# Loading q, k and v sixteen subtiles at a time instead of eight in an attention and gated feed-forward kernel

## The chip, the cores and the metric

The kernel runs on one core of a Trainium2 chip. The metric is the device time of one execution in microseconds (us), as a median over several runs, and less is better. TensorE is called PE, VectorE is DVE and ScalarE is ACT; POOL is GpSimd, which issues the loads, and SP issues the stores.

## The reference

The inputs are float32: q, k and v of 4 batches x 6336 rows x 256 channels, two 256 x 256 weights and a bias.

```
qn = q / (norm of q over the 6336 rows);  kn = k / (norm of k likewise)
a  = softmax(kn.T @ qn / tau)            # 256 x 256 for each batch
x  = v @ a
H  = relu(x @ w_h);  T = sigmoid(x @ w_t + b_t)
out = T * H + (1 - T) * x                # float32
```

All of q and k of a batch must be read before its 256 x 256 matrix is known; only then can the first row of that batch's output be made.

## The kernel before

A batch is cut into subtiles of 128 rows, 48 of them and a short tail of two. Each load is a cast from float32 in HBM to float16 in SBUF, of CH = 8 subtiles: 128 partitions x 8 x 256 x 4 bytes, 1.049 MB read, 8 KB in a row per partition. *Stage one* takes the subtiles of q and k of one batch and sums the products k.q, k.k and q.q in PSUM (for 40 subtiles of batches 1 to 3 the squares of q go to ACT and POOL instead). After the last of them a short chain makes the softmax and folds the weights into it. *Stage two* takes v of that batch in pairs of subtiles: transposes, then three groups of four matmuls (h, t and d), relu and gate on ACT, product and result on DVE, and a store for every eight subtiles. From then on PE mixes stage two of one batch with stage one of the next.

What runs when is decided while the kernel is built. A list scheduler in the kernel, called the planner below, plays the whole program through with a fixed duration for each instruction and two DMA queues, and issues instructions in the order that this gives. Its constants (priorities, when a load is due) were found by search.

```python
CH = 8
QK_BUFS = 5
V_BUFS = 5
UNTIL = 73      # stores are held back until this pair of stage two
AHEAD = 16      # transposing DMAs of the last batch, pairs ahead
V_AHEAD = 2
PRIO = {"tr": (24.974, 16.445, 34.195, 63.304), ...}   # 12 rows, cut
...
class Plan:
    RATE = 424e3
    ...
            act = [qq for qq in queues.values() if qq and qq[0][2] <= t + eps]
            share = self.RATE / max(1, len(act))     # an even share for each queue
...
    def load(nm, b, j, s, n):
        ...                                          # the tail, cut
        if s == 0:
            tiles[(nm, b, j)] = new(nm, [P, CH, C], f16, f"{nm}{b}_{j}")
        t = tiles[(nm, b, j)]
        nc.gpsimd.dma_start(
            out=t[:, s : s + n, :], in_=main_rows(src)[:, j * CH + s : j * CH + s + n, :]
        )
...
    seq = []                                         # the order of the loads
    for b in range(B):
        for j in range(NJ + 1):
            if (b, j) != (0, 0):
                seq.append((NP * b + CH // 2 * j - V_AHEAD, 1, "v", b, j))
            if b >= 1 and (b, j) != (1, 0):
                at = slot_of((b - 1) * NS + CH * j)
                seq.append((at, 0, "q", b, j))
                seq.append((at, 0, "k", b, j))
    seq.sort(key=lambda x: (x[0], x[1]))
    for _, _, nm, b, j in seq:
        plan_load(nm, b, j)
```

The loads go out in the order of `seq`. An instruction on a subtile waits for the load that brings it, and a buffer is free when its last subtile has been used.

## Time and profile before

| kernel before | |
|---|---|
| time, median of three runs | 270.38 us (270.2 to 270.92) |
| span of the profiled run | 268.3 us |
| PE busy | 246.4 us, 92% |
| ACT, DVE, POOL busy | 73%, 68%, 49% |
| main loads of q, k and v, in pieces | 80 |

The prediction shows the slices, the waits and PE's order. Two further views matter for it. The first line below is the first part of the page (busy us, share of the span, number of instructions); then comes the loads' queue from the third part (packets, MB, share of the 16 engines' span), and last two groups of DMA issues (count, KB each in SBUF or HBM, median us from issue to landing).

```profile
PE 246.4 (92%) x2430; PEld 216.6 (81%) x2430; DVE 181.6 (68%) x377; ACT 195.1 (73%) x365; POOL 131.7 (49%) x167
...
q0 software_dynamic: 13472, 39.20, 75.0%
...
out_dram<-o SPq DMA_DIRECT2D x23, 1024.0 KB, 9.6
v<-in_v_dram POOLq DMA_DIRECT2D x24, 512.0 KB, 16.6
```

PE has the smallest reserve. A load takes far longer to land (16.6 us) than it takes the queue to carry it (2.465 us, worked out in the prediction), because several stand in line.

### The profile page before, as it was taken

How to read it: one execution, taken by the hardware profiler on the slowest of the kernel's cores; microseconds unless marked ns; L12 is line 12 of the kernel's file. 1: busy time of each engine (PE TensorE's matmuls, PEld its weight loads, DVE VectorE, ACT ScalarE, POOL GpSimd, SP SyncE). 2: the span in 40 equal slices, each digit the busy share in tenths (PEclk: the TensorE clock that was granted, in tenths of full speed). 3: DMA queues.
4: the chain of work that ended last, by engine and by line, in shares of the span. 5: the costliest groups of instructions: out<-in, count | busy, mean ns of one | idle time of the engine just before them, and what ended most of it. 6: DMA issues, size and time to landing. Idle time of an engine off the chain costs nothing.

```text
span 268.3 us, 6249 instructions
## 1 busy us (share of the span) xinstructions
PE 246.4 (92%) x2430; PEld 216.6 (81%) x2430; DVE 181.6 (68%) x377; ACT 195.1 (73%) x365; POOL 131.7 (49%) x167
## 2 busy tenths in 40 slices
PE   0697977999999999999999999999999999999991
PEld 0596864889989978999999878999998778888880
DVE  1000035777766789557878797586878998998994
ACT  1001016978888789999898887787798999998980
POOL 7233468688778064695689138567655110000000
PEclk9999999999999999999999999999999999999998
DMA  6999999999999999999999999999999999999995
GB/s 107 215 211 208 206 206 202 212 213 214 214 213 212 213 214 255 247 263 269 275 286 258 267 267 254 249 236 281 287 280 239 284 214 304 379 399 165 351 423 232
DMA packets 24622, 67.24 MB, mean 251 GB/s; under 512 B 9104, under 2 KB 11280, under 8 KB 21648
## 3 DMA queue, kind: packets, MB, share of 16 engines
q0 software_dynamic: 13472, 39.20, 75.0%
q1 hardware_dynamic: 11120, 27.64, 29.0%
q8 instruction: 19, 0.31, 0.4%
q14 instruction: 11, 0.09, 0.1%
HBM read 78.38 MB, written 25.95 MB: 389 GB/s over the span
## 4 chain that ended last, share of the span: by engine, by line
PE 76%; DMA 12%; ACT 5%; POOL 2%; issue 2%; DVE 2%; ACTq 0%; DVEq 0%; POOLq 0%
PE h L800 16%; PE t L800 16%; PE d L800 15%; PE sg L452 12%; DMA k<-in_k_dram 10%; PE sg L453 6%; PE vtps L760 5%; DMA v<-in_v_dram 2%; ACT uu L854 2%; PE sg L455 2%; PE t L831 1%; PE vtps L754 1%; PE ah L689 1%; POOL q L327 1%; ACT d L840 1%
## 5 line engine op out<-in xcount | busy, mean ns | idle before, releaser
L800 PEld LDWEIGHTS <-vtsb 128*128 128x128 f16 (+1 forms) x1044 | 98.8, 99 | 17.3 <-issue 3.2
L452 PE MATMUL sg<-q,k 128*128 128x256 f16 x384 | 83.8, 277 | 12.7 <-DMA k<-in_k_dram 12.6
L861 DVE SCALAR_TENSOR_TENSOR pp<-uu,d 128x512 f32<-128x512 f32 (+1 forms) x100 | 68.0, 684 | 28.4 <-PE d L800 16.1
L453 PE MATMUL sg<-k 128*128 128x128 f16 x384 | 76.8, 223 | 0.0
L854 ACT ACTIVATE uu<-t 128x512 f32<-128x512 f32 (+1 forms) x100 | 59.7, 597 | 19.1 <-PE t L800 18.5
L880 DVE SCALAR_TENSOR_TENSOR o<-h,pp 128x512 f32<-128x512 f32 x96 | 65.5, 686 | 1.7
L840 ACT ACTIVATE d<-h 128x512 f32<-128x512 f32 (+1 forms) x100 | 57.9, 584 | 5.7 <-PE h L800 4.9
L800 PE MATMUL t<-mr,vtsb 128*128 128x256 f16 (+1 forms) x348 | 52.2, 272 | 1.5 <-ACT t L533 1.2
L800 PE MATMUL h<-mr,vtsb 128*128 128x256 f16 (+1 forms) x348 | 51.2, 272 | 0.5 <-ACT vtsb L533 0.5
L800 PE MATMUL d<-mr,vtsb 128*128 128x256 f16 (+1 forms) x348 | 51.5, 272 | 0.1
L452 PEld LDWEIGHTS <-k 128*128 128x128 f16 x384 | 38.0, 99 | 16.7 <-DMA k<-in_k_dram 13.9
L476 POOL TENSOR_TENSOR sq<-sq,sq 128x1024 f32<-128x1024 f32 x15 | 35.4, 2361 | 16.7 <-ACT sq L470 16.6
L453 PEld LDWEIGHTS <-k 128*128 128x128 f16 x384 | 38.0, 99 | 1.5
L533 ACT COPY t<-bias_all 128x512 f32<-128x512 f32 (+1 forms) x60 | 35.4, 591 | 1.4
L455 PE MATMUL sg<-q 128*128 128x128 f16 x144 | 32.5, 226 | 0.0
L470 ACT ACTIVATE sq<-q 128x1024 f32<-128x1024 f16 x30 | 31.3, 1053 | 0.0
L760 PE MATMUL vtps<-ident,v 128*128 128x128 f32 x144 | 27.8, 275 | 0.9 <-DMA v<-in_v_dram 0.6
L569 DVE SCALAR_TENSOR_TENSOR junk<-sg,ident 128x128 f32<-128x128 f32 x16 | 4.6, 288 | 33.2 <-PE sg L455 32.7
L535 DVE COPY vtsb<-vtps 128x256 f32<-128x256 f32 (+2 forms) x47 | 19.6, 418 | 7.0 <-PE vtps L760 6.7
L327 POOL DMA_DIRECT2D v<-in_v_dram x24 | 13.7, 571 | 18.9 <-PE vtps L760 11.7
L327 POOL DMA_DIRECT2D q<-in_q_dram x28 | 15.4, 552 | 15.1 <-DMA q<-in_q_dram 7.1
L327 POOL DMA_DIRECT2D k<-in_k_dram x28 | 15.3, 548 | 13.1 <-DMA k<-in_k_dram 9.2
(78 smaller groups left out, 249.5 us busy)
## 6 DMA issues: line engine op xcount, KB each, us to landing
out_dram<-o SPq DMA_DIRECT2D x23, 1024.0 KB, 9.6
v<-in_v_dram POOLq DMA_DIRECT2D x24, 512.0 KB, 16.6
q<-in_q_dram POOLq DMA_DIRECT2D x21, 512.0 KB, 16.2
k<-in_k_dram POOLq DMA_DIRECT2D x21, 512.0 KB, 18.0
q<-in_q_dram POOLq DMA_DIRECT2D x5, 256.0 KB, 9.6
k<-in_k_dram POOLq DMA_DIRECT2D x5, 256.0 KB, 8.9
out_dram<-o SPq DMA_DIRECT2D x2, 512.0 KB, 4.2
out_dram<-ot SPq DMA_DIRECT2D x4, 192.0 KB, 5.1
```

The costliest lines, as they stand in the source:

```text
L327: nc.gpsimd.dma_start(out=t[:, s : s + n, :], in_=main_rows(src)[:, j * CH + s : j * CH + s + n, :])
L452: nc.tensor.matmul(sg[c][:, 0:C], kc, qa, start=first, stop=False)
L453: nc.tensor.matmul(sg[c][:, C : C + P], kc, kc, start=False, stop=False)
L455: nc.tensor.matmul(sg[c][:, C + P : C + 2 * P], qa[:, cs], qa[:, cs], start=False, stop=last)
L476: add(out=sq, in0=sq, in1=other)
L533: nc.scalar.copy(out=out, in_=in_)
L760: nc.tensor.transpose(ps[:, u, 0:nr], v.bitcast(f32), ident0[0:nr, 0:nr])
L800: nc.tensor.matmul(out[0:nr, u, :], vt[u][kt][:, 0:nr], mr[kt][:, col * C : (col + 1) * C], **flags(u, kt))
L840: nc.scalar.activation(out=d[0:nr, :, :], in_=ps_t["h", b, i][0:nr, :, :], func=Act.Relu, scale=0.5)
L854: nc.scalar.activation(out=uu[0:nr, :, :], in_=ps_t.pop(("t", b, i))[0:nr, :, :], func=Act.Tanh, scale=-0.5)
L861: nc.vector.scalar_tensor_tensor(out=pp[0:nr, :, :], in0=el.pop(("uu", b, i))[0:nr, :, :], scalar=1.0, in1=ps_t.pop(("d", b, i))[0:nr, :, ...
L880: nc.vector.scalar_tensor_tensor(out=ot, in0=ps_t.pop(("h", b, i))[0:nr, :, :], scalar=0.0, in1=el.pop(("pp", b, i))[0:nr, :, :], op0=AluO ...
```

## The change

The intent: fewer, larger loads with longer rows. Each main load now brings LC = 16 subtiles, reads 2.097 MB and has 16 KB in a row per partition. Three buffers of 16 take the place of five of 8. The head (all of q and k of batch 0, the first eight subtiles of q and k of batch 1, the first eight of v) still comes in pieces of at most 8. All constants of the planner were searched anew.

```diff
+LC = 16
-QK_BUFS = 5
-V_BUFS = 5
+QK_BUFS = 3
+V_BUFS = 3
-UNTIL = 73
-AHEAD = 16
+UNTIL = 63
+AHEAD = 11
-V_AHEAD = 2
+V_AHEAD = 2.5
 PRIO = {
-    "tr": (24.974, 16.445, 34.195, 63.304),
+    "tr": (-3.282, -3.586, -4.565, -0.124),
...                                    (eleven more rows, all new; HEAD, TAIL and ENDS too)
-            tiles[(nm, b, j)] = new(nm, [P, CH, C], f16, f"{nm}{b}_{j}")
+            tiles[(nm, b, j)] = new(nm, [P, LC, C], f16, f"{nm}{b}_{j}")
...
-        for j in range(NJ + 1):
-            if (b, j) != (0, 0):
-                seq.append((NP * b + CH // 2 * j - V_AHEAD, 1, "v", b, j))
-            if b >= 1 and (b, j) != (1, 0):
-                at = slot_of((b - 1) * NS + CH * j)
-                seq.append((at, 0, "q", b, j))
-                seq.append((at, 0, "k", b, j))
+        for j in range(NL + 1):
+            s = CH if (b, j) == (0, 0) else 0
+            seq.append((NP * b + (LC * j + s) // 2 - V_AHEAD, 1, "v", b, j, s))
+            if b >= 1:
+                s = CH if (b, j) == (1, 0) else 0
+                at = slot_of((b - 1) * NS + LC * j + s)
+                seq.append((at, 0, "q", b, j, s))
+                seq.append((at, 0, "k", b, j, s))
...
-    for _, _, nm, b, j in seq:
-        plan_load(nm, b, j)
+    for _, _, nm, b, j, s in seq:
+        plan_load(nm, b, j, s, LC - s)
```

More of the change, by code (lines that the diff above doesn't have):

```diff
@@ L27 @@
 APART = 5
-V_AHEAD = 2
+V_AHEAD = 2.5
 PRIO = {
-    "tr": (24.974, 16.445, 34.195, 63.304),
-    "ev": (74.59, 73.008, 67.512, 50.704),
-    "h": (-53.39, -86.015, -64.208, -14.641),
-    "bias": (-28.394, 23.065, -1.772, 4.453),
-    "t": (4.111, -1.918, 67.766, 74.312),
-    "relu": (46.555, -20.175, -1.498, 14.915),
-    "x": (0.958, -19.433, 43.343, -6.4),
-    "gate": (-54.132, 37.28, -94.231, -112.222),
-    "prod": (-40.861, -10.819, -26.763, -55.482),
-    "res": (53.604, 18.42, 116.457, -9.113),
-    "s1": (117.419, 42.459, 84.45),
-    "sq": (-15.195, 72.384, 19.395),
+    "tr": (-3.282, -3.586, -4.565, -0.124),
+    "ev": (-5.167, 18.053, 2.859, 3.861),
+    "h": (-1.452, 1.255, 0.62, 0.556),
+    "bias": (0.123, 3.568, 2.664, -1.224),
+    "t": (0.41, -6.752, -6.651, 4.505),
+    "relu": (-0.38, -0.537, 0.533, 9.281),
+    "x": (-2.607, 1.406, -4.336, 2.432),
+    "gate": (4.912, 4.7, 2.362, -12.905),
+    "prod": (-10.208, -4.864, -4.947, -16.086),
+    "res": (-15.539, 3.312, -8.353, 6.716),
+    "s1": (2.894, 15.325, 6.393),
+    "sq": (-0.758, 4.066, 5.437),
 }
 POW = 0.75
-HEAD = 5.5
-TAIL = 66
+HEAD = 4
+TAIL = 63
 EV = BIAS = ("ACT", "DVE")
-ENDS = [18, 48.5, 62.25]
+ENDS = [15.75, 46.75, 59.75]
 class Ring:
@@ L249 @@
     NJ = S // CH
+    NL = S // LC
     TR = (N - P * S) // 2
@@ L318, in load @@
         src = src_of[nm][b]
-        if j == NJ:
+        if j == NL:
             t = new(f"tail_{nm}", [P, 2, C], f16, f"{nm}{b}_t")
@@ L324, in load @@
         if s == 0:
-            tiles[(nm, b, j)] = new(nm, [P, CH, C], f16, f"{nm}{b}_{j}")
+            tiles[(nm, b, j)] = new(nm, [P, LC, C], f16, f"{nm}{b}_{j}")
         t = tiles[(nm, b, j)]
         nc.gpsimd.dma_start(
-            out=t[:, s : s + n, :], in_=main_rows(src)[:, j * CH + s : j * CH + s + n, :]
+            out=t[:, s : s + n, :], in_=main_rows(src)[:, j * LC + s : j * LC + s + n, :]
         )
@@ L333, in sub @@
         if s < S:
-            return tiles[(nm, b, s // CH)][:, s % CH, :]
-        return tiles[(nm, b, NJ)][0:TR, s - S, :]
+            return tiles[(nm, b, s // LC)][:, s % LC, :]
+        return tiles[(nm, b, NL)][0:TR, s - S, :]
     def rows(s):
@@ L340, with plan_load @@
     ld = {}
-    def plan_load(nm, b, j, s=0, n=CH):
-        size = P * n * C * 4 if j < NJ else TR * 2 * C * 4
-        tag = nm if j < NJ else f"tail_{nm}"
+    def plan_load(nm, b, j, s=0, n=LC):
+        size = P * n * C * 4 if j < NL else TR * 2 * C * 4
+        tag = nm if j < NL else f"tail_{nm}"
         x = plan.add(
             "POOL", len(plan.tasks), 0.54, 0, [], lambda: load(nm, b, j, s, n),
-            take=[tag] if s == 0 else [], size=size * (1 if j < NJ and n > 2 else SHORT),
+            take=[tag] if s == 0 else [], size=size * (1 if j < NL and n > 2 else SHORT),
         )
@@ L355, in loaded @@
         if s >= S:
-            return [ld[(nm, b, NJ)][0]]
-        return [[x for x in ld[(nm, b, s // CH)] if x.first <= s % CH][-1]]
+            return [ld[(nm, b, NL)][0]]
+        return [[x for x in ld[(nm, b, s // LC)] if x.first <= s % LC][-1]]
     def drops(nm, b, s):
-        if s < S and s % CH == CH - 1:
-            return [(ld[(nm, b, s // CH)][0], nm)]
+        if s < S and s % LC == LC - 1:
+            return [(ld[(nm, b, s // LC)][0], nm)]
         if s == NS - 1:
-            return [(ld[(nm, b, NJ)][0], f"tail_{nm}")]
+            return [(ld[(nm, b, NL)][0], f"tail_{nm}")]
         return []
-    plan_load("q", 0, 0)
-    plan_load("k", 0, 0)
-    consts = plan.add("POOL", len(plan.tasks), 0.6, 1.5, [], constants)
-    consts.serial = True
-    for j in range(1, NJ - 2):
-        plan_load("q", 0, j)
-        plan_load("k", 0, j)
-        if j == 2:
-            for nm in "qk":
-                plan_load(nm, 0, NJ)
-            b_ld = [
-                plan.add("POOL", len(plan.tasks), 0.54, 0, [], lambda u=u: load_b(u), size=4000)
-                for u in range(2)
-            ]
-    for j, s, n in ((NJ - 2, 0, 4), (NJ - 2, 4, 4), (NJ - 1, 0, 4), (NJ - 1, 4, 2), (NJ - 1, 6, 2)):
-        plan_load("q", 0, j, s, n)
-        plan_load("k", 0, j, s, n)
+    for s in range(0, LC, CH):
+        plan_load("q", 0, 0, s, CH)
+        plan_load("k", 0, 0, s, CH)
+        if s == 0:
+            consts = plan.add("POOL", len(plan.tasks), 0.6, 1.5, [], constants)
+            consts.serial = True
+    for s in range(LC, S - LC, CH):
+        plan_load("q", 0, s // LC, s % LC, CH)
+        plan_load("k", 0, s // LC, s % LC, CH)
+    for nm in "qk":
+        plan_load(nm, 0, NL)
+    b_ld = [
+        plan.add("POOL", len(plan.tasks), 0.54, 0, [], lambda u=u: load_b(u), size=4000)
+        for u in range(2)
+    ]
+    for s, n in ((0, 8), (8, 4), (12, 2), (14, 2)):
+        plan_load("q", 0, NL - 1, s, n)
+        plan_load("k", 0, NL - 1, s, n)
     for s in range(0, CH, CH // 2):
@@ L394 @@
         x.late = 0.5
-    plan_load("v", 0, 0)
+    plan_load("v", 0, 0, 0, CH)
     ends = [(-1, HEAD)] + [(e, (n + 1) * NS) for n, e in enumerate(ENDS)]
@@ L433, in order_of @@
             return list(range(NS))
-        return [*range(3 * CH), *range(S, NS), *range(3 * CH, S)]
+        return [*range(S - LC), *range(S, NS), *range(S - LC, S)]
     def sg_tag(b, c):
@@ L468, in squares @@
         sq_t[b, j, half] = sq = new("sq", [P, CH // 2, C], f32, f"sq{b}_{j}_{half}")
-        qa = tiles[("q", b, j)][:, half * CH // 2 : (half + 1) * CH // 2, :]
+        s = CH * j + half * CH // 2
+        qa = tiles[("q", b, s // LC)][:, s % LC : s % LC + CH // 2, :]
         nc.scalar.activation(out=sq, in_=qa, func=Act.Square)
@@ L766, in transpose_chunk @@
         vt = new(tag, [P, n, 2, nr], f16, f"{tag}{b}_{j}")
-        src = tiles[("v", b, j)][0:nr, :, :].rearrange("p s c -> p (s c)")
+        s = j * CH % LC
+        src = tiles[("v", b, j * CH // LC)][0:nr, s : s + n, :].rearrange("p s c -> p (s c)")
         nc.sync.dma_start(out=vt.rearrange("c s kt n -> c (s kt) n"), in_=src, transpose=True)
@@ L944, in plan_stage1 @@
                 take=[sg_tag(b, n)] if n < 2 else [],
-                drop=([] if apart(b, s // CH) else drops("q", b, s)) + drops("k", b, s),
+                drop=([] if apart(b, s // LC * LC // CH) and s < S else drops("q", b, s)) + drops("k", b, s),
             )
             x.lat = x.pitch if n < NS - 1 else 0.66
-            if apart(b, s // CH) and s % CH == CH - 1:
-                plan.add("NONE", 0, 0, 0, [x] + part_ends[s // CH], None, drop=drops("q", b, s))
+            if s % LC == LC - 1 and apart(b, s // LC * LC // CH):
+                ends = [y for j in range(s // LC * LC // CH, s // CH + 1) for y in part_ends.get(j, [])]
+                plan.add("NONE", 0, 0, 0, [x] + ends, None, drop=drops("q", b, s))
             if n < 2:
```

## The prediction

> **What bounds the kernel now.** I read the page's slices first, then the waits, then TensorE (PE) in order of time around the first h product, then the DMA queue in short windows. Slices of the page:
>
> ```profile
> PE   0697977999999999999999999999999999999991
> DMA  6999999999999999999999999999999999999995
> GB/s 107 215 211 208 206 206 202 212 213 214 214 213 212 213 214 255 247 263 269 275 286 258 267 267 254 249 236 281 287 280 239 284 214 304 379 399 165 351 423 232
> ```
>
> Each digit is a fortieth of 268.3 us. PE is full from the seventh slice on; the DMA engines are full almost from start to end. GB/s counts what lands, and a load reads float32 and lands float16, so 213 landed is 426 read. Two resources are thus nearly used up at once, and what matters is whether PE ever lacks its data. Longest waits:
>
> ```profile
> PE sg L452 <- DMA k<-in_k_dram: 12.6, 5, 9.0
> ...
> PE vtps L760 <- DMA v<-in_v_dram: 0.6, 1, 0.6
> ```
>
> PE waits for q and k only at the head, while batch 0 streams in (9.0 us for the first pair of loads, 3.6 in the other four waits), and for v once. PE around the first product of the second stage:
>
> ```profile
> 44.77 0.41 PE L760 MATMUL vtps<-ident,v 128*128 128x128 f32 x2 [0.63 <-DMA v<-in_v_dram]
> 45.65 0.61 PE L800 MATMUL h<-mr,vtsb 128*128 128x256 f16 x4 [0.46 <-ACT vtsb L533]
> 46.10 0.60 PE L800 MATMUL t<-mr,vtsb 128*128 128x256 f16 x4
> ...
> 61.55 0.38 PE L760 MATMUL vtps<-ident,v 128*128 128x128 f32 x2
> 61.76 0.27 PE L452 MATMUL sg<-q,k 128*128 128x256 f16 x1
> ```
>
> The head ends at 45.65 us, when the first v has landed. From there PE works without a marked wait on a load until its last product at about 262.5. The later visible idle, from windows of 20 us, is 2.0 us in all (0.1 to 60, 0.2 to 80, 0.4 to 100, 0.9 between 140 and 160, 0.4 between 200 and 220). So any PE delay caused after 45.65 goes into the end, unless other gaps are given up for it.
>
> How the queue shares loads and stores, in windows of 1 us:
>
> ```profile
> 104.00:105.00 1.00, 1.00 (x12) 0.84 (x11) 1.00 (x3) 0.97 (x3) 0.58 (x1) 1.00 1.08 222
> ...
> 106.00:107.00 1.00, 1.00 (x11) 0.84 (x10) 1.00 (x3) 0.96 (x2) 1.00 (x1) 1.00 1.07 328
> ```
>
> The last number is GB/s. Loads alone land some 213. With a store under way the sum is 328: if the store takes s of 426, s + (426 - s)/2 = 328 gives s = 230, about half each. The store in question was issued at 101.04 and begins to show only after 105.
>
> **What the Trainium skill says.** "DMA: Bandwidth & Descriptors", section "Measured", gives 341 GB/s for a transfer of 1 MB and 425 for 16 MB. This trace disagrees for queued transfers: in the head, GpSimd's next issues, each held by an earlier load's landing, follow at 9.18, 11.70, 14.16, 16.59 and 19.04 us, so 9.86 / 4 = 2.465 us for a load that reads 1.049 MB, 425 GB/s. Loads of 1 MB that stand in line already run at the rate the page gives for 16 MB; rows of 16 KB instead of 8 KB have no rate left to win. Same page, "Queues, rings and completion order": an engine goes round-robin between queues "at packet granularity". The half each above, with 8 KB read per row in both queues, agrees. Same page, "Anatomy of one DMA": about 2.0 us fixed per transfer; here it is covered by the queue (the median v lands 16.6 us after issue), so fewer transfers save no such time.
>
> **The change, part by part.** The instruction orders of both kernels can be compared without running them.
> 1. *Issues.* Main loads fall from 28 + 28 + 24 = 80 to 19 + 19 + 13 = 51. At about 0.55 us each GpSimd saves 29 x 0.55 = 16 us of its 131.7. GpSimd is 49% busy and never the bound: 0 on the path.
> 2. *Work of PE.* Same matmuls, but 18 instead of 17 bias matmuls into t (TAIL 63 for 66). Counting an elementwise group of four products as 0.436 us and a bias matmul as about 0.2: +0.2 us. The vector and scalar work is the same within a few copies.
> 3. *Head.* Batch 0 is still loaded in pieces of 8, 4 and 2 subtiles, and the same bytes stand ahead of the first v: all q and k of batch 0, eight subtiles of q and k of batch 1, the weights. That v is now issued before the norm on GpSimd instead of after it (38.88), but it was the queue and not the issue that held it, so it lands at 44.6 again and the first h starts at 45.65 again: 0.
> 4. *After the head, the part that I think decides.* Order of loads before: v, q, k, v, q, k ... of 8 subtiles, 2.465 us each. Now, after v: 8 more of q and k (47.1, 49.6), 8 of v (52.0), then 16 each of q (57.0), k (61.9), v (66.8), q (71.8), k (76.7), v (81.6). PE in its new order, from 45.65: two and a half pairs (6 groups x 0.436 + 2 transposes x 0.215 = 3.0) bring it to 48.7, where it needs the k of 49.6: wait 0.9. Up to the first matmul on q and k subtile 16 it has 19 groups (8.28), 8 subtiles of stage one at 0.334 (2.67; four matmuls, from the trace) and 6 transposes (1.29): 12.2. So it is there at 45.65 + 0.9 + 12.2 = 58.8 and waits for k until 61.9. Before, PE at 61.9 had done 21 groups, 12 subtiles and 9 transposes; now 19, 8 and 6. Deficit: 2 x 0.436 + 4 x 0.334 + 3 x 0.215 = 2.9 us. Smaller loads gave PE both inputs alternately; the larger ones make it wait for a whole 16 of q and a whole 16 of k when it has v for the pairs only up to pair 7.
> 5. *Next loads.* After 61.9 some 5.2 us of work reach the need for v at 67.1 (lands 66.8); a further 9.6 reach k at 76.7 (lands 76.7); a further 5.6 reach v at 82.3 (81.6). No further wait, but no slack.
> 6. *Buffers.* Three of 16 hold 48 subtiles, five of 8 held 40: no less ahead on average. The hold on stores ends at pair 63 instead of 73, the transposing DMAs go out 11 pairs ahead instead of 16: with 1.4 us per pair near the end and a median landing of 6.1 us, 15 us is still enough.
>
> Sum: +2.9 + 0.2 = +3.1 us. Against it stand the gaps that PE has anyway: the same count of groups, subtiles and transposes from 45.65 to the end comes to about 210 us, while the trace takes 216.8; some 7 us are lost in small gaps while PE waits for ScalarE or VectorE. While PE starves, those two catch up, and the new order may have fewer such gaps. I credit 1 us (a choice, not a measurement): 270.4 + 3.1 - 1.0 = 272.5.
>
> **Rivals.**
> *The gaps decide.* The reordered priorities could win back two or three of the 7 us of small gaps and the 2.0 of visible idle; then starvation is covered: 268 to 270. For it: ScalarE and VectorE are at 73% and 68% over the span, with peaks near 90%, and order does matter. Against: the old order was tuned as well.
> *Loads push stores aside.* If engines alternate row by row, a load row of 16 KB against a store row of 8 KB leaves a store a third: a store of 1 MB takes 7.4 us instead of 5, after a longer wait for its turn. Stores landed in 9.5 us in the median and 18.0 at most; seven output buffers with five held leave about two chunks, some 17 us, for one to land. VectorE never waited for a store before; it might now: 274 to 277. Against: the load queue then runs dry sooner and gives the time back.
> *Nothing moves.* If the DMA total is the true bound (104.3 MB at 425 GB/s is 245 us, plus the transposing DMAs and the short pieces), a PE delay at 60 us is hidden behind stores at the end: 270. Against: stores catch up by 264 us, when PE is already done.
>
> **Range and chances.** The floor is head plus present work: 3 us better needs nearly half of the small gaps, so 2% faster (below 265.0) is hardly reachable: 4%. Slower by 2% (above 275.8) needs the starvation and a stall of stores together: 14%. The range runs from all starvation won back plus 2 us (268.5) to starvation plus some 3 us of stalls (276.0).
>
> **What would show it.** Step 4: a PE wait on the DMA of k near 59 to 62 us, of 2 to 3 us, and another below 1 us near 49. Step 3: first h at 45.6, within 0.5. Head and queue rate: still 213 GB/s landed between 46 and 95 us. Second rival: about 284 instead of 320 GB/s in windows where both queues run, stores landing later, VectorE's o waiting on the DMA of the output. If PE has no wait on loads after 50 us, or if the first h comes over 1 us earlier, my working is wrong.

## The result, and the profile after

The changed kernel takes 273.64 us in the median (273.38 to 274.37, four runs); the kernel before took 270.29 (269.63 to 270.92, four runs) beside it. The ratio is 1.0129, with a 95% interval from 1.0097 to 1.016. Ratios here are the mean time of one kernel's runs over that of the other's of the same rounds, so not quite the ratio of the medians quoted. The kernel became 1.3% slower.

The page after, in the same lines as for before:

```profile
PE 246.5 (91%) x2431; PEld 216.6 (80%) x2431; DVE 184.1 (68%) x379; ACT 196.1 (72%) x362; POOL 116.8 (43%) x138
...
q0 software_dynamic: 9296, 39.20, 71.9%
...
out_dram<-o SPq DMA_DIRECT2D x23, 1024.0 KB, 11.8
v<-in_v_dram POOLq DMA_DIRECT2D x11, 1024.0 KB, 29.9
```

POOL is 14.9 us less busy, and PE does the same work in the same busy time. Stores land 2.2 us later, and a load of 16 lands 29.9 us after its issue. So where did the 3.4 us of the span (268.3 to 271.7) come from? The wait of PE on k over the whole run (in us, times, longest) has gained two waits and 0.9 us over the line in the prediction (12.6, 5, 9.0); the one wait on v, 0.6 us, is gone:

```profile
PE sg L456 <- DMA k<-in_k_dram: 13.5, 7, 8.9
```

PE in order of time shows these two, and more. Columns are start, duration, instruction, and in brackets PE's idle time before it and what ended it:

```profile
46.08 0.60 PE L806 MATMUL h<-mr,vtsb 128*128 128x256 f16 x4
...
50.03 0.28 PE L456 MATMUL sg<-q,k 128*128 128x256 f16 x1 [0.41 <-DMA k<-in_k_dram]
...
54.91 0.44 PE L765 MATMUL vtps<-ident,v 128*128 128x128 f32 x2
55.51 0.60 PE L806 MATMUL t<-mr,vtsb 128*128 128x256 f16 x4 [0.16 <-ACT t L538]
...
56.82 0.38 PE L765 MATMUL vtps<-ident,v 128*128 128x128 f32 x2
57.48 0.60 PE L806 MATMUL t<-mr,vtsb 128*128 128x256 f16 x4 [0.28 <-ACT t L538]
58.26 0.60 PE L806 MATMUL d<-mr,vtsb 128*128 128x256 f16 x4 [0.19 <-ACT d L846]
...
59.44 0.60 PE L806 MATMUL t<-mr,vtsb 128*128 128x256 f16 x4
...
60.43 0.60 PE L806 MATMUL h<-mr,vtsb 128*128 128x256 f16 x4
61.57 0.28 PE L456 MATMUL sg<-q,k 128*128 128x256 f16 x1 [0.54 <-DMA k<-in_k_dram]
```

From 54.91 to 61.57 PE has no stage one to do: subtiles 8 to 15 of q and k of batch 1 are used up and 16 to 31 have not landed. In these 6.66 us it starts nine groups of four matmuls and two pairs of transposes, 9 x 0.436 + 2 x 0.215 = 4.35 us of work. Of the 2.3 us that are lost, 0.7 stand before 61.57, after the last group (60.43 + 0.44 = 60.87), where k is named; the other 1.6 are lost between groups of stage two. The trace marks three of these gaps, 0.63 us, and names ACT each time; that the unmarked rest is ACT's pace too is inferred (ACT is busy without a marked gap from 56.20 to 61.72).

The windows of 16 us (busy time and count of PE, PE's weight loads, DVE, ACT and POOL, then granted clock, DMA share and GB/s), first of before:

```profile
46.00:62.00 16.00, 15.91 (x152) 13.79 (x150) 10.83 (x19) 14.21 (x25) 11.86 (x15) 1.00 1.06 214
```

and of after:

```profile
46.00:62.00 16.00, 14.12 (x127) 11.49 (x126) 8.76 (x14) 13.72 (x24) 10.84 (x12) 1.00 1.06 218
...
110.00:111.00 1.00, 1.00 (x12) 0.93 (x10) 0.97 (x2) 0.69 (x2) 0.92 (x2) 1.00 1.03 295
111.00:112.00 1.00, 1.00 (x14) 0.97 (x11) 0.96 (x3) 0.79 (x2) 1.00 (x2) 1.00 1.04 303
...
113.00:114.00 1.00, 1.00 (x11) 0.94 (x10) 0.58 (x2) 0.97 (x3) 0.92 (x3) 1.00 1.02 279
```

PE is idle for 1.88 us of the 16 instead of 0.09. The DMA engines carry as much as before, 218 GB/s landed, so the bytes come as fast but in the wrong pieces. The last three lines have loads and stores under way together; the rivals of the prediction, below, come back to them.

To follow the loss I summed PE's matmuls at their pace in the trace (0.109 us for one of 256 columns, 0.056 of 128, 0.107 for a float32 transpose). The *lag* at a time is how much later the other kernel has started the same amount of this work as the kernel before had by then. Each value is a mean over the microsecond around the time given. All matmuls are in the traces (2430 before, 2431 after), but the order of work differs, so a value is good to about 0.5 us.

| time in the kernel before, us | 46 | 50 | 55 | 62 | 80 | 100 | 150 |
|---|---|---|---|---|---|---|---|
| lag of the changed kernel, us | 0.2 | 0.7 | 1.1 | 2.7 | 3.0 | 3.1 | 3.0 |

The loss arises between 46 and 62 us, and it is neither regained nor doubled. PE's last product comes 3.4 us later. Of before and then of after:

```profile
262.04 0.60 PE L800 MATMUL d<-mr,vT_t 128*96 128x256 f16 x4 [0.29 <-ACT d L840]
```

```profile
265.43 0.60 PE L806 MATMUL d<-mr,vT_t 128*96 128x256 f16 x4 [0.29 <-ACT d L846]
```

### The profile page after: what moved, and what is told of

The parts are those of the page before. It is cut to its first block, busy times and chain, and to the rows that moved or that the text cites. A ratio compares the mean times of both kernels' runs of the same rounds, so it can differ in the third digit from the quotient of the medians.

```text
span 271.7 us, 6186 instructions
## 1 busy us (share of the span) xinstructions
PE 246.5 (91%) x2431; PEld 216.6 (80%) x2431; DVE 184.1 (68%) x379; ACT 196.1 (72%) x362; POOL 116.8 (43%) x138
## 4 chain that ended last, share of the span: by engine, by line
PE 71%; DMA 13%; ACT 5%; DVE 5%; issue 2%; POOL 2%; DVEq 0%; ACTq 0%; POOLq 0%
PE t L806 15%; PE h L806 14%; PE d L806 14%; DMA k<-in_k_dram 13%; PE sg L456 11%; PE sg L457 6%; PE vtps L765 5%; DVE pp L867 2%; PE sg L459 2%; ACT uu L860 2%; ACT sq L475 1%; ACT t L538 1%; PE t L837 1%; DVE o L886 1%; PE vtps L759 1%
## 5 line engine op out<-in xcount | busy, mean ns | idle before, releaser
L456 PE MATMUL sg<-q,k 128*128 128x256 f16 x384 | 81.8, 275 | 13.5 <-DMA k<-in_k_dram 13.5
L457 PE MATMUL sg<-k 128*128 128x128 f16 x384 | 75.7, 222 | 0.0
L806 PE MATMUL h<-mr,vtsb 128*128 128x256 f16 (+1 forms) x348 | 51.8, 272 | 0.3 <-DVE o L886 0.3
L538 ACT COPY t<-bias_all 128x512 f32<-128x512 f32 (+1 forms) x64 | 37.7, 590 | 1.6
L475 ACT ACTIVATE sq<-q 128x1024 f32<-128x1024 f16 x30 | 30.7, 1049 | 0.0
L540 DVE COPY vtsb<-vtps 128x256 f32<-128x256 f32 (+2 forms) x53 | 22.1, 418 | 7.3 <-PE vtps L765 6.7
L911 ACT COPY bias_all<-bias_t 128x512 f32<-128x512 f32 x1 | 0.6, 586 | 27.3 <-PE bias_t L908 27.3
L765 PEld LDWEIGHTS vtps<-ident,v 128*128 128x128 f32 x144 | 17.1, 141 | 3.9 <-DVE vtsb L540 2.3
L484 POOL TENSOR_TENSOR sq<-sq 128x512 f32<-128x512 f32 x15 | 19.2, 1282 | 0.9
## 6 DMA issues: line engine op xcount, KB each, us to landing
out_dram<-o SPq DMA_DIRECT2D x23, 1024.0 KB, 11.8
v<-in_v_dram POOLq DMA_DIRECT2D x11, 1024.0 KB, 29.9
```

The lines of the kernel that those rows point to most:

```text
L456: nc.tensor.matmul(sg[c][:, 0:C], kc, qa, start=first, stop=False)
L457: nc.tensor.matmul(sg[c][:, C : C + P], kc, kc, start=False, stop=False)
L475: nc.scalar.activation(out=sq, in_=qa, func=Act.Square)
L538: nc.scalar.copy(out=out, in_=in_)
L765: nc.tensor.transpose(ps[:, u, 0:nr], v.bitcast(f32), ident0[0:nr, 0:nr])
L806: nc.tensor.matmul(out[0:nr, u, :], vt[u][kt][:, 0:nr], mr[kt][:, col * C : (col + 1) * C], **flags(u, kt))
```

## The experiments

Three theories were open. A, starvation: a load of 16 makes PE wait for a whole 16, or leaves it with one kind of work. B, constants: the planner's newly searched constants order the work less well, whatever the loads are. C, rows: rows of 16 KB crowd the stores. All runs gave right results.

### First set: smaller loads with the constants of the change

The kernel before took 270.04 us in the median of 11 runs here. The first kernel loads only q and k subtiles 16 to 31 of batch 1 and v 16 to 31 of batch 0 as two eights each, in turn:

```diff
-    seq.append((NP * b + (LC * j + s) // 2 - V_AHEAD, 1, "v", b, j, s))
+    for s in range(0, LC if j < NL else 1, CH if (b == 0 and j == 1 or (b, j) == (0, 0)) else LC):
+        ...                       # (0, 0, 0) is in the head; v with n = CH here, else LC - s0
+    for s in range(0, LC if j < NL else 1, CH if (b == 1 and j == 1 or (b, j) == (1, 0)) else LC):
+        ...                       # the same for q and k
```

> Changed kernel, with only q and k subtiles 16 to 31 of batch 1 and v subtiles 16 to 31 of batch 0 loaded as two pieces of 8 in turn (buffers of 16 and all constants kept; the planner orders the engines anew). Theory A (TensorE is starved because the loads after the head come as 16 of q, 16 of k, 16 of v): the late start of the matmul on q and k subtile 16 (61.6 us) moves to about 57, but the next loads of 16 (k at 76.7, v at 81.6 us) then bind, so only part of the 3.3 us comes back: 271.5 to 273. Theory B (the new priorities are worse, load size is innocent): unchanged, 273.3 to 274. Theory C (rows of 16 KB push stores aside): unchanged.

It took 273.14 us (273.03 to 273.33), ratio 1.0108 (1.0088 to 1.0128). By the time alone this decides nothing: it lies between the ranges of A (up to 273) and of B and C (from 273.3). Window and PE's order:

```profile
46.00:62.00 16.00, 15.67 (x152) 13.80 (x153) 9.52 (x16) 13.79 (x24) 11.90 (x13) 1.00 1.06 213
```

```profile
64.77 0.28 PE L458 MATMUL sg<-q,k 128*128 128x256 f16 x1 [0.28 <-DMA k<-in_k_dram]
...
73.86 0.60 PE L808 MATMUL t<-mr,vtsb 128*128 128x256 f16 x4 [0.49 <-ACT t L540]
...
75.82 0.60 PE L808 MATMUL t<-mr,vtsb 128*128 128x256 f16 x4 [0.43 <-ACT t L540]
...
77.19 0.27 PE L458 MATMUL sg<-q,k 128*128 128x256 f16 x1
```

The early loss is gone: PE is busy for 15.67 of the 16 us, and the lag at 62 us is 0.4 instead of 2.7. At 64.77 PE waits a little for the k of the second eight. The larger loss comes after it: the lag is 1.6 at 70 us and 3.1 at 75. From 71.44 to 77.19 PE again has no stage one, nine groups and gaps named after ACT, because the next k, a load of 16, lands only at 76.3. With all loads in eights (the third kernel below) the lag at 75 is 1.2. Taking the large load away from one place moved the loss to the next one.

The second kernel does the same for all of q and k of batch 1 and for v 0 to 31 of batch 0; only the two conditions differ:

```diff
-    ... CH if (b == 0 and j == 1 or (b, j) == (0, 0)) else LC     # v
-    ... CH if (b == 1 and j == 1 or (b, j) == (1, 0)) else LC     # q, k
+    ... CH if (b == 0 and j <= 1 or (b, j) == (0, 0)) else LC
+    ... CH if (b == 1 or (b, j) == (1, 0)) else LC
```

> Changed kernel, with all q and k of batch 1 and v subtiles 0 to 31 of batch 0 in pieces of 8; everything later still 16. Theory A: nearly all of the deficit goes, 270.3 to 271.3, and the result is some 3 us better than the changed kernel. Theory B: 273.3 to 274. Theory C: 273.3 to 274, since stores only start at about 104 us, when these loads are done.

It took 274.94 us, ratio 1.0173 (1.0153 to 1.0193), and every expectation was missed. The lag is 0.4 at 62 us and 1.8 at 100, but 4.0 at 130. The third loads everything in eights, into halves of buffers of 16:

```diff
-    ... CH if (b == 0 and j <= 1 or (b, j) == (0, 0)) else LC
-    ... CH if (b == 1 or (b, j) == (1, 0)) else LC
+    ... CH if True else LC
+    ... CH if True else LC
```

> Changed kernel with every load in pieces of 8, buffers of 16 and constants kept. Theory A: as the one with early pieces only, within 0.5 us (270.3 to 271.3). Theory B: 273.3 to 274. Theory C: the whole gain appears only here, and GB/s in windows where loads and stores both run returns from about 290 to about 325.

It took 277.92 us, ratio 1.0284 (1.0264 to 1.0305): missed by more. The lag is 0.3 at 62 us, 1.0 at 100 and 0.3 at 160: next to no loss for 160 us. It then grows to 5.8 at 260. Windows of the last part, of before and of this kernel, and the largest wait in that window of this kernel:

```profile
240.00:260.00 20.00, 20.00 (x181) 17.26 (x179) 18.56 (x30) 18.23 (x36) 0.00 (x0) 1.00 1.09 306
```

```profile
240.00:260.00 20.00, 18.84 (x164) 15.34 (x162) 18.01 (x29) 15.40 (x29) 0.00 (x0) 1.00 0.91 257
```

```profile
ACT uu L862 <- DVE pp L869: 4.2, 9, 0.8
```

All loads are in by then (POOL has stopped). What is lost is order on the engines: ACT waits for DVE 4.2 us, a wait that the kernel before does not have there. The likely reason is that the end of the program had been fitted to one pattern of loads, and another pattern spoils it; the third set tests this.

The fourth kernel tried to leave the plan alone. It keeps the changed kernel's instruction order and only sends the two large loads q and k 16 to 31 of batch 1 as q, k, q, k of eight:

```diff
+        parts = [(nm, s, n)]
+        if (nm, b, j) == ("q", 1, 1):
+            parts = [("q", 0, CH)]
+        if (nm, b, j) == ("k", 1, 1):
+            parts = [("k", 0, CH), ("q", CH, CH), ("k", CH, CH)]
+        for p, s, n in parts:
+            nc.gpsimd.dma_start(...)
```

> Changed kernel, plan and TensorE order untouched; only the transfer of q and k subtiles 16 to 31 of batch 1 goes out as q 8, k 8, q 8, k 8, so that the first k is there at about 57 instead of 61.6. Theory A in its plain form (the wait on k is what costs): the wait of 0.5 us and the 0.7 us gap before the matmul at 61.57 go, and no more, because in this order TensorE reaches it only at 60.9: 272.7 to 273.3. If the wait itself were the whole 3 us, 270.5 to 271.

It took 279.09 us, ratio 1.0329 (1.0308 to 1.0351), and it tests something else than it should. POOL's sum of squares in the changed kernel, and POOL in this one:

```profile
45.12 2.36 POOL L481 TENSOR_TENSOR sq<-sq,sq 128x1024 f32<-128x1024 f32 x1
```

```profile
47.38 0.53 POOL L335 DMA_DIRECT2D q<-in_q_dram  x1 [2.17 <-PE vtps L772]
49.61 0.53 POOL L335 DMA_DIRECT2D k<-in_k_dram  x1 [1.71 <-DMA k<-in_k_dram]
50.16 2.38 POOL L488 TENSOR_TENSOR sq<-sq,sq 128x1024 f32<-128x1024 f32 x1
```

The two further issues wait, one of them for an earlier load to land, and POOL does nothing behind them until they are out: the sum comes 5 us later. ACT's squares then wait for the buffer that it frees (up to 2.28 us), and PE waits 3.90 us for ACT before a t at 58.63. The run says nothing about starvation.

### Second set: loads and constants exchanged

The first set suggested that constants and loads belong together. So I crossed them (before: 270.04 us, 12 runs). First, the changed kernel's loads with the constants of before:

```diff
-UNTIL = 63
+UNTIL = 73
-    "tr": (-3.282, -3.586, -4.565, -0.124),
+    "tr": (24.974, 16.445, 34.195, 63.304),
...                       (all other constants likewise)
```

> Changed kernel (loads of 16, three buffers) with all priorities and plan constants of the kernel before. Theory A (loads of 16 starve TensorE after the head): the work of TensorE lags by 2 to 4 us at 62 us, as in the changed kernel; end 273 us or later. Theory B (the new constants are to blame for all): no early lag, 269.5 to 271.5.

It took 290.74 us, ratio 1.0752 (1.0723 to 1.0782), as theory A said. The lag at 62 us is 2.6, as with the new constants; it is 17.3 at 240. Then the reverse, the kernel before with the constants of the change:

```diff
-UNTIL = 73
+UNTIL = 63
-    "tr": (24.974, 16.445, 34.195, 63.304),
+    "tr": (-3.282, -3.586, -4.565, -0.124),
...                       (all other constants likewise)
```

> Kernel before (loads of 8, five buffers) with the priorities and constants of the changed kernel. Theory A: no early lag (under 1 us at 62 us); the end is open, since the all-8 run has shown that these constants lose about 6 us after 200 us with loads of 8: 271 to 278. Theory B: an early lag of about 3 us at 62 us, 273 to 274.

It took 278.82 us, ratio 1.0332 (1.03 to 1.0364), with a lag at 62 us of 0.7. The early lag is A's; the end lies a little above both ranges. Eights in buffers of 16 with the constants of before:

```diff
 # everything in eights, as above
-UNTIL = 63
+UNTIL = 73
...                       (all other constants of before)
```

> Loads of 8 in three buffers of 16, all constants of the kernel before: only the buffers differ from the kernel before (and the pieces at the end of batch 0). Theory A: no early lag, 269.5 to 271.5, so that buffers of 16 cost nothing by themselves. Rival (a buffer of 16 is freed late and that costs): 272 or more, with a lag that grows after 80 us.

It took 286.61 us, ratio 1.0605 (1.0582 to 1.0629), with a lag of 1.0 at 62 us; it loses most after 240 us, where PE is busy for 14.75 of 20. Taken by the time this is what the rival forecast; the first kernel of the third set, with the same loads and buffers and its own constants, speaks against it. The last keeps loads of 8 and all constants of before, but sends the six early loads of subtiles 16 to 31 in the order q q k k v v, to imitate the order of large loads without large loads:

```diff
     seq.sort(key=lambda x: (x[0], x[1]))
+    early = [x for x in seq if (x[3] == (0 if x[2] == "v" else 1)) and 2 <= x[4] < 4]
+    first = min(seq.index(x) for x in early)
+    rest = [x for x in seq[first:] if x not in early]
+    seq = seq[:first] + sorted(early, key=lambda x: (x[4] // 2, "qkv".index(x[2]), x[4])) + rest
```

> Kernel before, loads still of 8 with 8 KB rows, all constants kept; only the order of six loads changes: subtiles 16 to 31 as q q k k v v instead of q k v q k v. Theory A (what costs is the time at which the k comes, not the row): the lag at 62 to 65 us is 1.5 to 3 us, end 271.5 to 273.5. Rival (16 KB rows or the new constants): 269.5 to 270.7, as before.

It took 284.03 us, ratio 1.0505 (1.0461 to 1.0549), a miss for both: the lag is only 0.7 at 62 us and 0.6 at 80, and the bulk is lost after 210. The imitation was weak. The k of subtile 16 landed at 59.9 us, against 57.3 before but 61.5 in the changed kernel. So no run shows that the order without the large loads makes the whole early loss.

Two things follow. The end times of this set, and of the second and third kernel before it, can't be read as the price of load sizes: a pattern of loads that meets constants searched for another pattern lost 4 to 18 us after 62 us. The early window can be read, since the late part has no say in it: with loads of 16 the lag at 62 us is 2.7 and 2.6 under the two sets of constants, and with loads of 8 it is 0.3 to 1.0 under both. These constants alone (theory B) therefore do not explain the early loss of the changed kernel. For the end time a fair comparison was still missing.

### Third set: constants searched for each pattern

I searched constants for each pattern of loads in the same way, for the earliest end that the kernel's own planner computes. This planner knows nothing of row lengths: it gives each queue an even share. The kernel before took 270.41 us in the median of 11 runs of this set.

First, everything in eights, in buffers of 16:

```diff
 # everything in eights, as above
-AHEAD = 11
+AHEAD = 15
-V_AHEAD = 2.5
+V_AHEAD = 5.5
-    "tr": (-3.282, -3.586, -4.565, -0.124),
+    "tr": (-8.356, 50.339, -68.388, 90.324),
...                       (eleven more rows; HEAD, TAIL and ENDS too)
```

> Loads of 8 in three buffers of 16, priorities and constants searched anew for this pattern against the end that the kernel's own planner computes (265.95; that figure is 267.09 for the kernel before, 269.74 for the changed one, and the eight runs that went through the planner so far measured 3.1 to 6.2 us above it). Theory A (loads of 16 cost, whatever the constants): 269.0 to 270.6, as good as before or a little better, and TensorE's work at 62 us within 1 us of before. Theory B (the new constants were merely worse tuned): this says nothing against it, but then the 16-load kernel retuned in the same way must come down as far.

Then the changed kernel's loads, searched again from several starts, of which the best was taken:

```diff
-UNTIL = 63
-AHEAD = 11
+UNTIL = 64
+AHEAD = 6
-V_AHEAD = 2.5
+V_AHEAD = 2.0
...                       (PRIO, HEAD and ENDS too)
```

> The changed kernel, loads of 16 as they are, constants searched in the same way and for longer (best of four searches from four starts; planner's end 269.36). Theory A: 272.6 to 273.6, so retuning does not help, and the lag at 62 us stays 2 to 3 us. Theory B: under 271.

Then eights for q and k of batch 1 and for v 0 to 31 of batch 0, and sixteens after that:

```diff
 # the early eights, as above
-V_AHEAD = 2.5
+V_AHEAD = 9.5
...                       (all other constants searched too)
```

> Pieces of 8 only for q and k of batch 1 and v subtiles 0 to 31 of batch 0, everything later 16, constants searched in the same way (planner's end 268.92). My first form of theory A (only the loads right after the head matter): 270 to 271. The other form (each load of 16 until the stores have drained costs in its turn): 272 to 273, early lag below 1 us and a second deficit of about 2 us later, before 180 us.

And the kernel before, searched again:

```diff
-UNTIL = 73
-AHEAD = 16
+UNTIL = 61
+AHEAD = 21
-V_AHEAD = 2
+V_AHEAD = 4.5
...                       (all other constants searched too)
```

> Kernel before (loads of 8, five buffers of 8) with constants searched in the same way (planner's end 266.41 against 267.09): 269.3 to 270.8. With the first run of this set it tells whether buffers of 16 are worth anything when loads stay at 8: if so, that one is faster by 0.3 us or more.

Each ratio is against the kernel before; in the last column is the end that the planner computes, a number that steered the search and not a measurement.

| loads, constants searched anew | median, us | ratio (95%) | lag at 62 us | planner, us |
|---|---|---|---|---|
| all 8, buffers of 16 | 270.75 (269.25 to 272.0) | 0.9996 (0.9954 to 1.0037) | 0.9 | 265.95 |
| all 16 after the head | 273.9 (273.17 to 274.15) | 1.0116 (1.0082 to 1.015) | 3.0 | 269.36 |
| 8 early, then 16 | 272.64 (271.81 to 272.97) | 1.007 (1.0033 to 1.0108) | 1.8 | 268.92 |
| 8, the kernel before | 269.93 (269.47 to 270.75) | 0.9978 (0.9943 to 1.0013) | 0.2 | 266.41 |

The first kernel came out 0.15 us and the second 0.3 us above what theory A expected; the second is far above the 271 of theory B. With constants fitted in the same way, loads of 8 are where the kernel before was, and loads of 16 are 1.2% slower: 273.9 - 270.75 = 3.15 us between the first two rows, which have the same buffers and differ in the size of the loads and in the constants found for it. The planner's ends differ by 3.4. It has no notion of rows or of unequal shares, so what it does model (a load is usable when all of it has landed, a buffer is free when all of it has been used, the order on the engines) can account for the whole difference. This argument is coarse, as the four kernels measured 3.5 to 4.8 us above the planner's end. The lag says it better. The first store goes out at 104.7 us in the changed kernel and at 103.5 in the second row's, where the lag at 100 us is already 3.1 and 3.5. Rows that crowd the stores (theory C) can't have made that part, and at most some tenths are left for them in the changed kernel, whose last product is 3.4 late.

PE's order and window in the second row's kernel, and the window of the first row's:

```profile
61.78 0.28 PE L456 MATMUL sg<-q,k 128*128 128x256 f16 x1 [0.46 <-DMA k<-in_k_dram]
```

```profile
46.00:62.00 16.00, 13.93 (x125) 11.57 (x126) 9.37 (x16) 13.44 (x23) 11.34 (x11) 1.00 1.06 218
```

```profile
46.00:62.00 16.00, 15.02 (x143) 13.32 (x144) 11.47 (x21) 13.21 (x24) 12.52 (x13) 1.00 1.06 213
```

The new search, with another order, has kept the same hole: PE reaches the k of subtile 16 near 61.8 us and waits, and it is idle for 2.07 us of the 16, against 0.98 with eights. The third row's kernel missed its expectation of a lag below 1 us at 62: it has 1.8 there, 1.4 at 110 and 3.0 at 140. Its loads up to 62 us are all eights, so size is not the cause of that early lag. The search brought three loads of v (44.4, 46.9 and 49.4) before the next q and k (51.9 and 54.3), and the lag, 0.9 at 46, is 2.3 at 55. A lag at 62 us is thus no proof of large loads by itself. In the changed kernel the first large loads after the head are the place where the loss shows, but not the only place where large loads cost: with those in eights, 0.7% remain.

The first row narrows the price down. Its buffers of 16 are also given back only after a whole 16, and it is level with the kernel before, so late giving back by itself costs nothing that these runs resolve (the interval allows 0.4%). Nor do such buffers gain anything with loads of 8: the first row was to be faster than the last by 0.3 us or more if they did, and it is not.

What stays open: how the later loss of the third row comes about. And a kernel with 16 KB rows but the landing times of eights, or with 8 KB rows in the order of sixteens, would test the rows alone; none was run (the last kernel of the second set came only part of the way). And no version beats the kernel before: the first and the last row are level with it within their intervals.

## Why the prediction was right or wrong

The direction and the place held, and the size in part: 272.5 was predicted and 273.64 measured, inside the range of 268.5 to 276; of the 3.35 us measured, 2.1 were forecast. Step by step:

1. *Issues.* Right. POOL fell by 14.9 us (16 predicted), and nothing on the path moved for it.
2. *Work of PE.* Right: 246.5 us busy against 246.4.
3. *Head.* Nearly right. The first h came at 46.08 instead of 45.65, within the 0.5 allowed. In the new order two pairs of transposes stand before it, and the second waited 0.96 us for DVE's copy.
4. *After the head.* Right in cause and sum, wrong in how it would look. The deficit at 62 us was 2.7 (2.9 predicted), and it appears with loads of 16 under each of the three sets of constants tried (2.7, 2.6 and 3.0). The first wait was 0.41 and not 0.9, since PE came at 49.6 and not at 48.7. The second was to be a visible wait of "2 to 3 us" from 58.8; it was 0.54. The term that failed is the time of PE's arrival, "45.65 + 0.9 + 12.2 = 58.8". I had counted the 19 groups at PE's full pace of 0.436. With no stage one between them, three groups of stage two took 1.96 us (the t at 55.51, 57.48 and 59.44) instead of the 1.3 to 1.5 of PE's full pace, with gaps that are named after ACT where the trace marks them; so PE came at 60.9. The starvation was spread over gaps named after ACT and only its rest stood before k. It is the same hole: k landed at 61.5 (61.9 predicted), and stage one could not go on before.
5. *Next loads.* Right. PE has no further wait on a load after 61.57, and the lag stays near 3.
6. *Buffers.* Right: the transposing DMAs came in time, and the first row of the third set shows no cost of buffers of 16 with loads of 8.

The sum was 3.1 us, and the medians differ by 3.35. The credit of 1 us for small gaps, called a choice, was wrong: without it the prediction would have been 273.5. The idea behind it was that DVE and ACT would catch up while PE starves. ACT was not idle in that stretch: it was busy for 13.72 us of the 16 (14.21 before), and PE waited for it. Two readings of the prediction are slightly off: the seventh slice of PE holds only 7 tenths, so PE is full from the eighth; and all of PE's matmuls from 45.65 on come to 208 us at their pace and not 210, so the small gaps are some 9 us and not 7.

The rivals. *The gaps decide* did not happen. *Loads push stores aside*: the mechanism is in the trace, the cost is not. With both queues busy the seven windows from 109 to 116 us show 279 to 303 GB/s, where the kernel before had 315 to 328 from 105 to 109. From s + (426 - s)/2 = 279 a store gets s = 132 of 426, 31%, and from 303 it gets 42%, around the third (284 GB/s) that was predicted. Stores land later (11.8 for 9.6 us), but neither DVE nor ACT has a wait on a DMA in the list of waits; that the output buffers took it up is inferred. *Nothing moves* is refuted by the last product, which came 3.4 us later and took the end with it.

## What to carry to other kernels

Where loads stand in line at full rate already, as here (214 and 218 GB/s landed), a larger load brings no more bytes per second, and it makes the consumer wait for a larger whole: with several streams through one queue, grain can decide whether an engine always has both kinds of work. A starved engine need not show a wait on the load; it can show as an engine that runs one kind of work at the pace of its slower partner, so compare the work done by a given time. Where the order was searched for one pattern of transfers, compare patterns only after an equal search for each.

## What the Trainium skill lacked or had wrong

- "DMA: Bandwidth & Descriptors", section "Measured": 341 GB/s for 1 MB, 425 for 16 MB. Here loads that read 1.049 MB and stood in line took 2.465 us each, 425 GB/s, and loads twice as large came about as fast (218 against 214 GB/s landed, a load landing half of what it reads). The table does not say whether its figures are for a transfer alone. Its columns do not fit together either: 1 MB in its 6.15 us is 170 GB/s and 16 MB in its 79.0 us is 212, each half of the rate beside it, so what its GB/s count is not clear, and the likeness of our 425 to its 425 may be chance.
- The same page, section "Rules for kernel authors", asks for 1 MiB or more per DMA for the most bandwidth, and that rule sets no upper size and says nothing of the time to first use. Here 2 MB instead of 1 MB cost 1.2 to 1.3%.
- The same page, section "Queues, rings and completion order", has engines alternate between queues packet by packet, but does not say what shares follow. With 8 KB rows in both queues a store had about half (328 GB/s landed in all); with 16 KB rows in the loads alone it had some 31 to 42% (279 to 303).
- No page that I found gives the cost of issuing loads from GpSimd while it also computes, when an issue has to wait. With two further issues waiting in its order, its sum of squares began at 50.16 instead of 45.12 us, and PE waited 3.90 us in the end.
